# A tuned retention and SwiGLU kernel on one core: the last part of each h block moves from GpSimd to VectorE, the decays of k to ScalarE, and one silu into a PSUM bank

## The chip, the cores and the metric

The kernel runs on one core of a Trainium2 chip. The metric is the device time of one execution in microseconds (us). The kernel before was timed three times: 715.64, 715.67 and 717.3 us, median 715.67 us. One more execution was recorded by the hardware profiler; its span is 716.6 us, and all positions below ("at 374.96 us") count from the start of that span.

The engines are named as in the profile: PE is TensorE (its matmuls; PEld its weight loads), DVE is VectorE, ACT is ScalarE, POOL is GpSimd, SP issues most of the DMAs. Each engine works through its own instructions in order; semaphores tie the engines together.

## The reference

Two blocks, one behind the other, all in fp32.

```
B, H, S, D = 4, 8, 768, 64
gamma = 1 - 2 ** (-5 - h)                       # one decay per head
state = gamma * state + outer(k[t], v[t])       # per batch and head, D x D
y[t]  = (1 / sqrt(D)) * q[t] @ state            # over t = 0 .. S-1
x     = y as (B*S, H*D) = (3072, 512)
out   = (silu(x @ w_gate) * (x @ w_val)) @ w_out    # d_ff = 1536
```

## The kernel before

**Attention in chunks.** A sequence of 768 steps is cut into six chunks of 128. Inside a chunk the recurrence is a masked product of q and k, weighted by powers of gamma; between chunks a state of 64 x 64 per head is carried. For the state, k of the chunk is multiplied row by row by a decay that depends on the row and the head (`scale_k2`, the table `kdec`: 128 rows x 8 heads, each value good for 64 columns). For the part that reads the old state, q is multiplied by another table (`scale_q2`: one of the two chunks of a pair on VectorE, the other on GpSimd).

**Segments and stages.** The tokens are worked in four segments; a segment holds three chunks of each of two sequences, 768 tokens. A segment has an *up* stage (x times gate and value weights, silu, product: the hidden activations, kept transposed in `hT` as 12 blocks f of 128 rows x 2 x 384 tokens) and a *down* stage (the 12 blocks times w_out, summed up over f in six PSUM banks, one for each 128 tokens). Beside the matmuls of a down stage runs the attention of the next segment: three pairs of chunks p = 0, 1, 2, each with the parts s (scores, twice), m (mix with the own chunk), o (mix with the other half, then y is copied out of PSUM) and t (new state). The last down stage has no next segment.

**Parts of fp32.** Matmuls after the first up stage run on numbers rounded to a shorter mantissa. To keep fp32 accuracy each operand is split in three parts, and three passes are summed. A *near* split has three steps on three engines: `near_a` on ScalarE makes the rounded part, `near_b` on VectorE subtracts it from the operand, `near_c` on GpSimd adds the two parts into the third. It serves the weights of the up stages (`weights`) and the blocks of `hT` in the down stages (`h_split`). A *far* split (`far_a` to `far_d`) serves x and w_out; w_out is split once, in the first down stage (`w_load`, with `far_b` on GpSimd), and read back ready afterwards. The up product uses seven products instead of eight (a Strassen scheme over the two sequences, the two halves of d_model, and gate and value), which is why copies and sums of PSUM banks stand between the products.

**Order.** Nothing is scheduled by a machine at run time. Each step is entered with a due time, `at(t, fn, ...)`; `run` sorts all steps by due time and emits them in that order, so each engine's queue is the order of the due times. `down_stage` sets the due times of a down stage, `up3` those of an up stage from the second segment on. In `h_split` a block that TensorE needs at t has its three steps due at t - 7.5, t - 6.3 and t - 5.2.

**Lines that the change touches.** L538 is the POOL product of `scale_k2`. L663 is the POOL add of `near_c` (for weights and for h). L80 is the helper `both`, a VectorE instruction with two inputs; many steps are recorded there, the product `hT <- hT, tmp` of `up3` among them. `c11` in `up3` lies in `tmp` in SBUF; banks 0, 1, 6 and 7 are the PSUM banks that an up stage uses, banks 0 to 5 are those that a down stage sums in, 6 and 7 serve the attention.

Of the kernel before, what the change touches and what calls it, by code (L numbers as in the profile page):

```python
# [14 lines left out]
AF = mybir.ActivationFunctionType  # L15
ALU = mybir.AluOpType

P = 128
B, H, S, D = 4, 8, 768, 64
# [7 lines left out]
TH = L * P  # L27
# [18 lines left out]
ONE = 4095.0  # L46
# [3 lines left out]
def tile_retnet_swiglu(  # L50
# [22 lines left out]
    add, mul, sub = ALU.add, ALU.mult, ALU.subtract  # L73
    tt, stt, pool = (nc.vector.tensor_tensor, nc.vector.scalar_tensor_tensor,
                     nc.gpsimd.tensor_tensor)
    act, copy = nc.scalar.activation, nc.scalar.copy
# [8 lines left out]
    def f32(t):  # L85
        return t.bitcast(F32)
# [3 lines left out]
    hT = consts.tile([P, NF, 2, TH], F32, name="hT")  # L90
# [25 lines left out]
    banks = [psum.tile([P, 512], F32, name=f"bank{i}") for i in range(8)]  # L116
# [4 lines left out]
    def at(t, fn, *args, **kw):  # L121
        events.append((t, len(events), lambda: fn(*args, **kw)))  # L122
# [213 lines left out]
    kdec = tab[:, KDEC0:GDEC0]  # L336
# [90 lines left out]
    kdec_b = tab[:, ds(2 * TA, H)]  # L427
# [106 lines left out]

    def scale_k2(p, i):
        kd = given[p][3][i].rearrange("p (h d) -> p h d", h=H)
        dec = (kdec_b if i else kdec)[:, :, None].to_broadcast([P, H, D])
        pool(kd, kd, dec, op=mul)  # L538

    def new_states(s, p):  # L540
        ci = seg_chunks(s)[2 * p] % NCK
# [106 lines left out]
    def item(kind, n):  # L648
        k = turns[kind]
        turns[kind] += 1  # L650
        slots = {"g": 4, "o": 3}[kind]
        t = place(f"{kind}item{k}", {"g": 3 * 2 * TH, "o": 3 * DM}[kind], R12,
                  tag=f"{kind}{k % slots}")
        return t[:, : 3 * n].rearrange("p (a b) -> p a b", a=3)

    def near_a(o, x):
        act(o[0], x, AF.Copy, scale=CUT / FAR)  # L657

    def near_b(o, x):
        stt(o[1], f32(o[0]), -FAR, x, op0=mul, op1=add)  # L660

    def near_c(o):
        pool(o[2], f32(o[0]), f32(o[1]), op=add)  # L663

    def far_a(o, x):
        act(o[0], x, AF.Copy, scale=CUT)
# [10 lines left out]
    def near(t, o, x, n_a, n_b, n_c):  # L677
        o = o()
        at(t + n_a, lambda: near_a(o, x))
        at(t + n_b, lambda: near_b(o, x))  # L680
        at(t + n_c, lambda: near_c(o))
# [63 lines left out]
    def weights(t, f, g):  # L745
        it = {}
        if f == 0:
            t -= 1.8

        def begin():  # L750
            it["o"] = group(f, g)
            near_a(*it["o"])

        at(t - 7.2, begin)
        at(t - 5.6, lambda: near_b(*it["o"]))
        at(t - 4.4, lambda: near_c(it["o"][0]))
# [11 lines left out]
    def up3(s, f, t):  # L768
        x, z, wb = (banks[i][:, :TH] for i in (6 + f % 2, 0, 1))
        p1, u2, p5 = (tmp[:, ts(i, TH)] for i in range(3))  # L770
        c11 = tmp[:, ts(3 + f % 2, TH)]
        for g, first in enumerate((0, 3, 6)):
            weights(t + first * PROD, f, g)
        for n, p in enumerate(ORDER):
            o = {1: x, 6: x, 7: x, 4: x, 2: z, 5: wb, 3: wb}[p]
            at(t + n * PROD, product, s, f, p, o, p in (1, 2, 5))
        e = lambda n: t + (n + 1) * PROD + 0.1
        at(e(0), copy, p1, x)
        at(e(1), tt, c11, z, p1, op=add)
        at(e(1) + 0.7, act, c11, c11, AF.Silu, scale=ONE)  # L780
        at(e(2), copy, u2, x)
        at(e(3), copy, p5, wb)
        at(e(4), tt, hT[:, f, 1], x, p5, op=add)
        at(e(5), tt, hT[:, f, 0], wb, u2, op=add)
        at(e(5) + 0.7, both, hT[:, f, 0], hT[:, f, 0], c11, mul)
        at(e(6), act, x, x, AF.Silu, scale=ONE)
        at(e(6) + 0.7, tt, hT[:, f, 1], hT[:, f, 1], x, op=mul)

# [4 lines left out]
    def h_split(t, f):  # L793
        it = {}

        def begin():
            hs[f] = item("g", 2 * TH)
            it["o"] = [hs[f][:, i] for i in range(3)]
            near_a(it["o"], hT[:, f].rearrange("p i t -> p (i t)"))

        at(t - 7.5, begin)
        at(t - 6.3, lambda: near_b(it["o"], hT[:, f].rearrange("p i t -> p (i t)")))
        at(t - 5.2, lambda: near_c(it["o"]))

    def w_load(t, s, f):
        raw_w = chunk_x[:, ds(NC * 2 * P + f % 2 * DM, DM)]
# [50 lines left out]
    def down_stage(s, t, first_order=range(6), between=None):  # L857
        nxt = s + 1 if s + 1 < NSEG else None
        slot_at, steps = [], []
        for n in range(6 * NF):  # L860
# [4 lines left out]
            if nxt and n in PARTS:  # L865
# [3 lines left out]
                if what == "s":  # L869
                    at(t, scores_of, p, g)  # L870
                    for i in range(2):
                        at(d, decayed, p, g, i)
                    if g and ci:
                        for i in range(2):
                            at(d, scale_q2, p, i)
                elif what == "m":
                    at(t, mix_own, nxt, p)
                    at(d, fence)
                    if ci < NCK - 1:
                        for i in range(2):  # L880
                            at(d, scale_k2, p, i)
                elif what == "o":
                    at(t, mix_other, nxt, p)
                    if p == 0:
                        at(t, begin_x, nxt)
                    for c in range(2):
                        for i in range(2):
                            for hh in range(2):
                                at(d, bring_y, hh, i, c)
                    if ci < NCK - 1:  # L890
                        at(d + 2.4, decay2, nxt, p)
                    make_x(d + 2.6, nxt, p)
                elif ci < NCK - 1:
                    at(t, state2, nxt, p)
                    at(d, keep_state, nxt, p)
# [9 lines left out]
        for f in range(NF):  # L905
            h_split(steps[f], f)
            w_load(steps[f], s, f)
# [65 lines left out]
    t = down_stage(0, end, (0, 4, 3, 2, 5, 1), last_gates)  # L973
    for s in range(1, NSEG):
        for f in range(NF):
            up3(s, f, t + UPT * f)
            if f > 2:
                at(t + UPT * (f - 1) - 2.5, load_unit, f)
        t += NF * UPT
        if s + 1 < NSEG:  # L980
            for n in range(5):
                at(t - (18, 13, 12, 5, 4)[n], load_pair, s + 1, n)
        t = down_stage(s, t)
# [52 lines left out]
```

## Time and profile before

| what | before |
|---|---|
| time, median of 3 | 715.67 us |
| span of the profiled execution | 716.6 us |
| PE busy | 673.5 us (94%) |
| DVE busy | 496.8 us (69%) |
| ACT busy | 364.0 us (51%) |
| POOL busy | 355.9 us (50%) |
| mean granted TensorE clock | 0.982 of full speed |

How to read the profile's lines. A line of the table of stages gives a stretch in us, its length, the busy time and number of instructions of each engine in it, the granted TensorE clock, and the DMA. A line of the timeline gives start, duration, engine, line of the kernel, operation, output and inputs with their shapes, and in brackets how long the engine had been idle before it and who ended that. A line of the groups gives line, engine, operation, names, shapes, count, then busy time and mean duration in ns, then the idle time ahead of it. The first 143 us hold the attention of the first segment and its up stage, which the change does not touch; the four down stages begin near 143, 326, 493 and 663 us, the three later up stages near 240, 403 and 572 us.

### The profile page before, as it was taken

To read this page: it belongs to the slowest core of one execution; us is meant where nothing else is said; L and a number is where in the kernel's file an instruction comes from. 1 tells how busy PE (TensorE), PEld (TensorE's weight loads), DVE (VectorE), ACT (ScalarE), POOL (GpSimd) and SP (SyncE) were. 2 spreads that over 40 slices of the span, in tenths; PEclk is the share of its full clock that TensorE was granted. 3 is DMA by queue.
4 is the path that set the end of the run, shared out by engine and by line. 5 is a ranking of instruction groups with operands and counts; after the bars stand their busy time and mean duration, and the time that the engine had idled before them with its cause. 6 is when DMAs were issued, how large, how long until landed. Compare 5 with 4: busy or idle time off the path is not lost.

```text
span 716.6 us, 12389 instructions
## 1 busy us (share of the span) xinstructions
PE 673.5 (94%) x4724; PEld 553.9 (77%) x4724; DVE 496.8 (69%) x730; ACT 364.0 (51%) x693; POOL 355.9 (50%) x226
## 2 busy tenths in 40 slices
PE   7998999997878999999989899999998899999997
PEld 6754555566666899997667799998776699999886
DVE  3888998777788676774765767766566766777421
ACT  2668787525646555551545554553442655554211
POOL 0434444565745555664345555554453455665540
PEclk9999999999989999999999999999999999999999
DMA  9796898966565533265765443254755544232564
GB/s 313 255 371 223 239 394 346 291 241 206 189 228 207 192 114 144 87 217 162 248 206 206 157 148 110 102 184 151 235 183 191 192 160 141 103 103 88 178 202 150
DMA packets 51739, 140.80 MB, mean 196 GB/s; under 512 B 6368, under 2 KB 19168, under 8 KB 51680
## 3 DMA queue, kind: packets, MB, share of 16 engines
q1 hardware_dynamic: 48224, 133.72, 54.5%
q10 hardware_dynamic: 3456, 6.29, 2.5%
q8 instruction: 37, 0.61, 0.4%
q14 instruction: 22, 0.18, 0.1%
HBM read 110.11 MB, written 29.88 MB: 195 GB/s over the span
## 4 chain that ended last, share of the span: by engine, by line
PE 68%; DVE 13%; ACT 6%; issue 4%; POOL 3%; DMA 1%; ACTq 0%; SPq 0%; DVEq 0%; POOLq 0%
PE bank L764 36%; PE bank L830 15%; PE bank L600 12%; PE bank L458 5%; ACT chunk_x L695 3%; DVE x L80 3%; DVE gitem L660 2%; DVE tmp L80 2%; DVE x L672 1%; ACT gitem L657 1%; POOL gitem L663 1%; POOL first L252 1%; DVE chunk_x L841 1%; DMA loads<-in_k_n_dram 1%; DVE tmp L477 1%
## 5 line engine op out<-in xcount | busy, mean ns | idle before, releaser
L663 POOL TENSOR_TENSOR gitem<-gitem 128x768 fp32r<-128x768 f32 x120 | 228.1, 1901 | 183.7 <-DVE gitem L660 170.7
L764 PE MATMUL bank<-x,gitem 128*128 128x384 f32 x1296 | 239.8, 342 | 6.7 <-ACT tmp L122 6.2
L764 PEld LDWEIGHTS bank<-x,gitem 128*128 128x128 f32 x1296 | 226.0, 190 | 15.3 <-ACT tmp L122 7.9
L830 PE MATMUL bank<-oitem,gitem 128*128 128x512 f32 x864 | 216.4, 405 | 3.8 <-ACT oitem L675 3.2
L830 PEld LDWEIGHTS bank<-oitem,gitem 128*128 128x128 f32 x864 | 162.9, 193 | 43.2 <-issue 6.5
L660 DVE SCALAR_TENSOR_TENSOR gitem<-gitem,loads 128x768 fp32r<-128x768 f32 x72 | 81.2, 1127 | 60.9 <-ACT gitem L657 60.9
L600 PE MATMUL bank<-first 128*128 128x384 f32 x336 | 111.2, 489 | 2.6 <-DVE hT L635 1.6
L600 PEld LDWEIGHTS bank<-first 128*128 128x128 f32 x336 | 62.8, 190 | 49.0 <-DVE hT L635 2.2
L660 DVE SCALAR_TENSOR_TENSOR gitem<-gitem,hT 128x768 fp32r<-128x768 f32 x48 | 55.8, 1164 | 46.4 <-ACT gitem L657 46.2
L252 POOL TENSOR_TENSOR first<-first,rawp 128x1024 int32<-128x1024 int32 (+1 forms) x21 | 40.0, 1919 | 58.5 <-DVE first L242 31.5
L657 ACT ACTIVATE gitem<-loads 128x768 fp32r<-128x768 f32 x72 | 60.7, 843 | 2.9 <-DVE oitem L660 2.9
L122 ACT ACTIVATE bank<-bank 128x384 f32<-128x384 f32 x36 | 17.1, 475 | 73.8 <-PE bank L764 73.8
L695 ACT COPY chunk_x<-bank 64x256 f32<-64x256 f32 x72 | 26.4, 367 | 54.3 <-PE bank L458 53.4
L122 ACT COPY tmp<-bank 128x384 f32<-128x384 f32 x108 | 50.6, 469 | 3.7 <-PE bank L764 3.6
L657 ACT ACTIVATE gitem<-hT 128x768 fp32r<-128x768 f32 x48 | 39.5, 836 | 25.0 <-PE bank L830 24.9
L122 DVE TENSOR_TENSOR hT<-bank,tmp 128x384 f32<-128x384 f32 x72 | 39.8, 554 | 17.3 <-PE bank L764 17.3
L764 PE MATMUL bank<-x,oitem 128*128 128x384 f32 x216 | 44.8, 342 | 0.4 <-DVE hT L122 0.4
L458 PEld LDWEIGHTS bank<-loads 64*64 64x64 f32 (+1 forms) x800 | 23.9, 141 | 26.1 <-DVE tmp L477 12.4
L122 ACT ACTIVATE tmp<-tmp 128x384 f32<-128x384 f32 x36 | 18.9, 526 | 48.7 <-DVE tmp L122 48.7
L458 PE MATMUL bank<-loads 64*64 64x64 f32 (+2 forms) x800 | 29.0, 253 | 15.0 <-DVE tmp L477 8.6
L663 POOL TENSOR_TENSOR oitem<-oitem 128x256 fp32r<-128x256 f32 x36 | 26.6, 739 | 30.5 <-DVE oitem L660 30.5
L764 PEld LDWEIGHTS bank<-x,oitem 128*128 128x128 f32 x216 | 36.3, 188 | 3.3 <-DVE hT L122 0.7
(97 smaller groups left out, 699.6 us busy)
## 6 DMA issues: line engine op xcount, KB each, us to landing
loads<-wup SPq DMA_DIRECT2D x36, 896.0 KB, 4.7
oitem<-wdnt SPq DMA_DIRECT2D x36, 768.0 KB, 4.4
wup<-first SPq DMA_DIRECT2D x12, 896.0 KB, 8.8
wdnt<-oitem SPq DMA_DIRECT2D x12, 768.0 KB, 4.5
rawp<-in_w_val_dram SPq DMA_DIRECT2D x24, 256.0 KB, 5.8
rawp<-in_w_gate_dram SPq DMA_DIRECT2D x12, 512.0 KB, 6.5
out_dram<-chunk_x ACTq DMA_DIRECT2D x24, 256.0 KB, 2.1
loads<-in_k_t_dram SPq DMA_DIRECT2D x18, 256.0 KB, 3.7
```

The lines of the kernel that those rows point to most:

```text
L80: stt(o, x, 1.0, y, op0=mul, op1=op)
L122: events.append((t, len(events), lambda: fn(*args, **kw)))
L252: pool(d[:, ts(i, n)].bitcast(I32), d[:, ts(i, n)].bitcast(I32), lo[:, ts(i, n)].bitcast(I32), op=add)
L458: nc.tensor.matmul(o, a, b, start=start, stop=True, skip_group_check=True)
L477: tt(att[p, g, i], banks[R0 + i][:, :TA], side[g][:, i], op=mul)
L600: nc.tensor.matmul(o, w[:, slot, k], a[:, k], start=(start and k == 0), stop=(stop and k == KH - 1), skip_group_check=True)
L657: act(o[0], x, AF.Copy, scale=CUT / FAR)
L660: stt(o[1], f32(o[0]), -FAR, x, op0=mul, op1=add)
L663: pool(o[2], f32(o[0]), f32(o[1]), op=add)
L695: copy(cx[half[i], ds(2 * h, 2), c], y_both(h, i, c))
L764: nc.tensor.matmul(o, w[:, a, k], xs_of[s][:, a, OP[p], k], start=start and a == k == 0, stop=a == 2 and k == KH - 1, skip_group_check=True)
L830: nc.tensor.matmul(banks[tok], hs[f][:, a, ds(i * TH + u * P, P)], wo[f][:, a], start=f == a == 0, stop=f == NF - 1 and a == 2, skip_group ...
```

## The change

It makes three edits.

1. The third step of each split of an h block (`near_c` in `h_split`) runs on VectorE instead of GpSimd, and is due 0.1 us earlier. There are 12 blocks in each of four down stages, 48 in all. For the weights it stays on GpSimd.
2. The decays of k (`scale_k2`) become eight ScalarE copies with a per-row scale, one for each head, instead of one GpSimd product; 14 products become 112 copies.
3. In the later up stages silu of `c11` writes into a PSUM bank that the stage does not use (banks 2 and 3, in turn for even and odd f), and the product that follows reads it from there. Before, silu was written over `c11` in SBUF, and the product had both inputs in SBUF.

The purpose is to take work off GpSimd, and to have fewer VectorE instructions that read two operands from SBUF.

```diff
     def scale_k2(p, i):
         kd = given[p][3][i].rearrange("p (h d) -> p h d", h=H)
-        dec = (kdec_b if i else kdec)[:, :, None].to_broadcast([P, H, D])
-        pool(kd, kd, dec, op=mul)
+        dec = kdec_b if i else kdec
+        for h in range(H):
+            act(kd[:, h], kd[:, h], AF.Copy, scale=dec[:, ds(h, 1)])
...
-    def near_c(o):
-        pool(o[2], f32(o[0]), f32(o[1]), op=add)
+    def near_c(o, op=pool):
+        op(o[2], f32(o[0]), f32(o[1]), op=add)
...
         c11 = tmp[:, ts(3 + f % 2, TH)]
+        gate = banks[2 + f % 2][:, :TH]
...
-        at(e(1) + 0.7, act, c11, c11, AF.Silu, scale=ONE)
+        at(e(1) + 0.7, act, gate, c11, AF.Silu, scale=ONE)
...
-        at(e(5) + 0.7, both, hT[:, f, 0], hT[:, f, 0], c11, mul)
+        at(e(5) + 0.7, tt, hT[:, f, 0], hT[:, f, 0], gate, op=mul)
...
-        at(t - 5.2, lambda: near_c(it["o"]))
+        at(t - 5.3, lambda: near_c(it["o"], both))
```

## The prediction

> **What bounds the kernel now.** I read the busy times first, then a table by stage, then the PE timeline of the down stages for its idle time, and last the DVE and POOL timelines at those moments. Busy time on the page:
>
> ```profile
> PE 673.5 (94%) x4724; PEld 553.9 (77%) x4724; DVE 496.8 (69%) x730; ACT 364.0 (51%) x693; POOL 355.9 (50%) x226
> ```
>
> TensorE leaves 43 us, of which 5 are start-up (25.80 busy of the first 31 us). The table by stage says where the rest is:
>
> ```profile
> 143.00:240.00 97.00, 82.21 (x797) 63.42 (x796) 75.29 (x91) 49.75 (x95) 56.60 (x35) 0.93 0.62 217
> 240.00:326.00 86.00, 85.63 (x481) 81.92 (x480) 62.11 (x93) 44.58 (x92) 49.34 (x34) 1.00 0.42 143
> 326.00:403.00 77.00, 71.30 (x772) 55.28 (x770) 50.43 (x69) 34.97 (x68) 37.00 (x22) 1.00 0.59 197
> 493.00:572.00 79.00, 72.86 (x772) 56.39 (x770) 53.24 (x70) 33.95 (x66) 35.45 (x20) 0.98 0.55 188
> ```
>
> The up stages (second row) are full: PE 85.63 of 86, nothing to win there. The first three down stages, D0, D1 and D2, have 14.8, 5.7 and 6.1 us of idle PE. That is the most an edit of the other engines can give, apart from a slower clock behind long stalls. In D1 the PE timeline shows each stall with who ended it:
>
> ```profile
> 328.19 0.99 PE L458 MATMUL bank<-loads 64*64 64x128 f32 x30 [0.60 <-DVE hT L122]
> 352.26 1.35 PE L458 MATMUL bank<-loads 64*64 64x128 f32 x32 [0.94 <-DVE tmp L477]
> 358.12 0.55 PE L458 MATMUL bank<-loads,states 64*64 64x128 f32 x11 [0.52 <-POOL loads L531]
> 374.96 1.35 PE L458 MATMUL bank<-loads 64*64 64x128 f32 x32 [1.89 <-DVE tmp L477]
> ```
>
> These are attention parts that wait for DVE to empty a bank (L477), or for the scaled q (L531). DVE does it late because it is held in the instruction before. Ahead of the 374.96 stall:
>
> ```profile
> 371.58 2.86 DVE L80 SCALAR_TENSOR_TENSOR x<-x,tmp 128x1024 fp32r<-128x1024 f32 x1
> 374.36 1.01 DVE L477 TENSOR_TENSOR tmp<-bank,tab 128x384 f32<-128x384 f32 x2
> 371.47 1.89 POOL L663 TENSOR_TENSOR gitem<-gitem 128x768 fp32r<-128x768 f32 x1 [6.15 <-DVE gitem L660]
> ```
>
> The same L80 form has a median of 1.22 us; here it takes 2.86, as it began 0.11 us after a POOL add and ran on its own pace once that ended at 373.36. So a POOL instruction costs DVE up to its whole duration. A stall of 1.9 to 3.8 us is also followed by a slow clock; for the one at 543.52 us in D2:
>
> ```profile
> 540.00:545.00 5.00, 3.07 (x40) 2.11 (x38) 5.00 (x5) 0.42 (x1) 1.88 (x1) 0.95 0.71 231
> 545.00:551.00 6.00, 6.00 (x54) 4.73 (x55) 2.79 (x5) 2.52 (x3) 3.14 (x2) 0.76 0.46 151
> ```
>
> At 0.76 for 6 us some 1.4 us of matmul work are lost on top of the 1.90 us stall.
>
> **What the Trainium skill says.** "SBUF — State Buffer", section "Who interferes with whom": "A DVE instruction with two SBUF inputs contends with a GpSimd instruction that reads SBUF", and the second to issue is fully blocked. The trace agrees: the product hT <- hT,tmp (L80, both inputs in SBUF) takes 557 ns at its least and 1031 in the mean, while the same 384 columns with one input in PSUM (L122) take 542, and 555 at most. "ScalarE: Activation LUTs", section "What ACT_TABLE_LOAD costs", prices an ACTIVATE at 186 ns + 0.833 per column, + 93 for a per-row operand, with 93 ns of overlap back to back: for 64 columns 332 and a pitch of 239. The trace has this form at L380, 334 ns; its pitch is seen at L549 (128 columns, 389 ns, four in 1.28 us: 297), which less 64 x 0.833 gives 244. "TensorE: Matmul & The Clock Gate", part 1, puts the clock at half after an idle window of about 3.4 us; the trace has dips already behind 1.90 us, so I take its own.
>
> **The change, part by part.**
>
> *near_c of h on DVE.* It removes 48 POOL adds of 1.84 us (12 a stage) and adds 48 DVE instructions of 768 columns with two SBUF inputs; the equal form is near_b (L660), 0.95 us, 0.88 as pitch since neighbours overlap. So DVE gets 12 x 0.88 = 10.5 us more in a stage. What it gets back is the blocking by those adds: in D1 the excess over the least duration of each form is 1.5 (345.86), 0.5 (355.52), 1.1 (356.86), 0.6 (360.04), 1.6 (371.58), 0.3 (381.81), 1.1 (390.61), together 6.7 us. DVE busy in D1 rises from 50.4 to about 54 of 77 us: not a bound. What matters is where the instructions stand ahead of a stall. From the instruction order of the changed kernel, stall by stage:
> D1: at 328.19 two near_c stand shortly ahead of the last product of the up stage, one of them directly, against a product at 325.76 that took 1.91 and will take 0.55 (edit 3): -0.5. At 352.26 the burst loses 1.54 and gets one near_c of 0.88: -0.7. At 358.12 the scaled q waited behind a POOL near_c of 2.71, gone: -0.5. At 374.96 the L80 loses 1.64, and the near_c of that block is queued behind L477, not ahead: -1.6. Sum -3.3.
> D2 has the same four (0.62; 1.30 behind the new state; 0.51; 1.90): -0.5, -0.7, -0.5, -1.65, and without the last stall the clock dip of 1.4 should go: -4.7.
> D0 keeps 12 POOL adds for w_out (L669), which go on blocking. Stalls 3.55, 1.59, 1.13, 3.83 and 3.23 us: the first is neutral (1.5 of blocking less at 169.37, 0.88 of near_c and up to 0.8 of ScalarE delay more), then -0.7, -0.8, -1.6 (L80 at 200.56 took 2.82, with near_c again behind L477), -0.7. The dip behind the fourth, 0.62 over 9 us or 3.4 us of work, may shrink: I take -1.2. At the start of D0 near_c of block 0 now stands in DVE's queue ahead of L635 and L638, for which a product waits: +0.7. Sum -4.3.
> D3 has no attention and a full PE: 0.
> The wait that each near_c adds is for near_b just ahead on the same engine; behind it are the sums of x, then L477 and the new state, for which PE waits; counted above.
>
> *Decays on ScalarE.* 7 pairs of chunks x 16 copies x 0.244 = 3.9 us of ScalarE each, 27 us in all (between 239 and 334 ns a copy: 27 and 37). POOL loses 14 x 1.365 = 19 us. They stand behind a near_a, ahead of the y copies (L695). Before those ScalarE idles 12.8, 5.9 and 5.8 us in D1, 13.6 and 5.9 in D2, and 4.0 us before the far_d at 188.29 in D0: there they are hidden at no cost. Two tight places: D0, first pair, y copies 0.8 us later (counted), and D1, third pair, where k is issued at 376.4 to 377.9 and lands (median 4.0 us) near 381.5, with copies to about 384.3 and a near_a behind, against 384.86: 0 to 1 us, I take 0.
>
> *silu into PSUM.* Silu costs 482 instead of 526 ns (the first up stage has the form bank<-tmp, L612); the product 0.55 instead of 1.03, 36 times, 17 us of DVE in full up stages: nothing on the path but the 0.5 counted. Banks 2 and 3 are free there: the last product is read before the down stage reaches its fourth token block (329 us against 326.3).
>
> The sum is -12.3, 703.4 us. Removed stalls rarely come in full, as PE arriving earlier meets the next wait (transfers, y copies), and the two down-to-up turns (2.41 and 2.96 us of stall) hang on a DVE burst whose length stays (-1.07 +0.88). I take three quarters: -9.2, **706.5 us**.
>
> **Rivals.**
> *A, full gain or more* (chance 0.22): all dips but those at the turns go, D0's fourth stall with them: 715.7 - 12.3 - 3 = 700.4 us. For it: the dips follow stalls that lose most of their length. Against: D0's keep 2 us and more.
> *B, little moves* (0.16): the stalls are ended by something else right behind, y copies or far_d: the two L477 stalls of D1 and D2 alone give -3.5: 712 us. For it: ACT's waits in D0 (28.2 us for DVE at L675) remain. Against: at 374.96 nothing but DVE's queue holds PE.
> *C, slower* (0.07): near_c is on the path in each of the nine attention pairs, 9 x 0.88 = 8 us, of which relief pays 4, and the ScalarE copies delay y by 1 us in two: 715.7 + 8 - 4 + 2 = 722 us. For it: DVE is already busy 6 of 7 us around the stalls. Against: four of the stalls have it behind L477.
> *The forecast* has 0.55.
>
> **How the numbers follow.** Faster by over 0.3% means under 713.5: the forecast, A, and most of B, 0.55 + 0.22 + 0.10 = 0.87; same 0.06 from the rest of B; slower 0.07 from C. The range leaves out the far half of A and all of C: 700.5 to 714 us.
>
> **What would show it.** POOL busy down by about 48 x 1.9 + 19 = 110 us to 246; DVE about 48 x 0.95 - 17 - 20 (three stages like D1's 6.7) = 9 up, near 505; ACT 35 up. L80 hT gone as a group, its successor at 0.55 us. L80 x<-x,tmp at 1.22 in D1 and D2. PE idle under 3 us in D1 before the turn; no dip in D2 before 560 us. It is wrong if L477 or the new state still holds PE for over 1 us in D1 and D2 (rival C, or B if near_c is not what stands before it), or if L695 starts over 1 us after its part o.

## The result, and the profile after

| | before | after |
|---|---|---|
| median of 4 runs, same chip | 716.48 us (715.64 to 717.88) | 704.96 us (704.16 to 707.31) |
| ratio, 95% interval | | 0.9843 [0.9812, 0.9873] |
| span of the profiled execution | 716.6 us | 702.4 us |

The changed kernel is 1.6% faster. The two profiled executions lie further apart (14.2 us) than the medians (11.5 us): by the timer, the profiled execution of the kernel before took 718.37 us, above its median, and that of the changed kernel 704.16, its shortest. Their mean granted clocks, 0.982 and 0.989, lie further apart than those of the timed runs too (median 0.986 over 19 further runs of the kernel before, 0.985 to 0.989 in the four of the changed one). Shares of stages below are read from the profiles, gains of versions from the timed runs.

Busy times, from the page of the changed kernel:

```profile
PE 664.6 (95%) x4724; PEld 552.3 (79%) x4724; DVE 496.8 (71%) x778; ACT 391.4 (56%) x805; POOL 247.9 (35%) x164
```

GpSimd loses 108 us. VectorE has 48 instructions more and is busy for exactly as long as before. TensorE has the same 4,724 matmuls, and is "busy" 8.9 us less.

The table by stage of the changed kernel (stretch, length, then PE, PEld, DVE, ACT, POOL, granted clock, DMA), D0, D1, D2:

```profile
143.00:236.00 93.00, 80.11 (x794) 60.78 (x793) 77.10 (x103) 57.05 (x127) 28.64 (x19) 0.96 0.65 225
322.00:396.00 74.00, 70.33 (x769) 54.62 (x767) 52.93 (x80) 46.52 (x116) 9.46 (x5) 1.00 0.61 207
486.00:560.00 74.00, 69.42 (x767) 54.32 (x766) 53.09 (x80) 40.81 (x97) 10.73 (x6) 1.00 0.60 203
```

In D1 and D2 GpSimd has 5 and 6 instructions left, of 22 and 20. Idle PE in D1 is 3.7 us where it was 5.7, and half of that is the turn into the next up stage. The stalls of D1, from the PE timeline:

```profile
346.54 1.35 PE L458 MATMUL bank<-loads 64*64 64x128 f32 x32 [0.28 <-DVE tmp L477]
352.62 0.67 PE L458 MATMUL bank<-loads,states 64*64 64x128 f32 x16 [1.10 <-DVE loads L80]
367.81 1.35 PE L458 MATMUL bank<-loads 64*64 64x128 f32 x32 [0.25 <-DVE tmp L477]
```

They answer one by one to the lines of before: 0.60 gone, 0.94 now 0.28, 0.52 now 1.10 and ended by VectorE instead of GpSimd, 1.89 now 0.25. The groups of the changed kernel that the edits touch:

```profile
L80 DVE SCALAR_TENSOR_TENSOR gitem<-gitem 128x768 fp32r<-128x768 f32 x48 | 51.4, 1072 | 1.0
L539 ACT ACTIVATE loads<-loads,tab 128x64 f32<-128x64 f32 x112 | 27.5, 334 | 0.9 <-DMA loads<-in_k_n_dram 0.9
L80 DVE SCALAR_TENSOR_TENSOR x<-x,tmp 128x1024 fp32r<-128x1024 f32 x9 | 11.0, 1218 | 0.0
```

The last row is the held instruction of the prediction. The same row in the kernel before:

```profile
L80 DVE SCALAR_TENSOR_TENSOR x<-x,tmp 128x1024 fp32r<-128x1024 f32 x9 | 15.8, 1761 | 0.0
```

Its mean fell from 1761 ns to the undisturbed 1218. The 72 adds that GpSimd keeps are those of the weights.

The length of each stage, taken from the starts of its first matmul and of the next stage's first, says where the 14.2 us are:

| us | D0 | U1 | D1 | U2 | D2 | U3 | one block in the middle of U | last block of U |
|---|---|---|---|---|---|---|---|---|
| before | 89.28 | 91.32 | 73.36 | 93.75 | 75.07 | 95.14 | 7.50 | 7.4 to 7.5 |
| after | 85.46 | 90.37 | 70.79 | 92.66 | 70.93 | 93.43 | 7.29 to 7.31 | 8.0 to 8.1 |

Down stages: 10.5 us. Up stages: 3.75 us, where none had been expected. The first 145 us and the last down stage differ by 0.1 us together.

Part of the 10.5 us is TensorE's clock. Multiplied by the length of its stretch, what the granted clock lacks to 1.00 in the tables by stage is 6.8 us in D0 and 1.6 in D2 before, and 3.7 and 0 after. So up to 4.7 us of these two gains (an estimate from the tables) come from fewer spells of slow clock. D1 has none in either kernel; its 2.6 us are shorter waits alone.

### The profile page after: what moved, and what is told of

Same layout as the page of the kernel before. It is cut to its first block, busy times and chain, and to the rows that moved or that the text cites. A ratio compares the mean times of both kernels' runs of the same rounds, so it can differ in the third digit from the quotient of the medians.

```text
span 702.4 us, 12451 instructions
## 1 busy us (share of the span) xinstructions
PE 664.6 (95%) x4724; PEld 552.3 (79%) x4724; DVE 496.8 (71%) x778; ACT 391.4 (56%) x805; POOL 247.9 (35%) x164
## 4 chain that ended last, share of the span: by engine, by line
PE 63%; DVE 16%; ACT 8%; DMA 6%; issue 4%; SPq 1%; POOL 0%; ACTq 0%; DVEq 0%; POOLq 0%
PE bank L765 35%; PE bank L832 15%; PE bank L601 9%; PE bank L458 4%; DVE gitem L661 3%; ACT chunk_x L696 3%; DVE x L673 2%; DVE x L80 2%; ACT gitem L658 2%; DVE gitem L80 1%; DVE tmp L80 1%; DMA loads<-in_v_n_dram 1%; DVE tmp L477 1%; DVE first L80 1%; DMA rawp<-in_q_t_dram 1%
## 5 line engine op out<-in xcount | busy, mean ns | idle before, releaser
L765 PE MATMUL bank<-x,gitem 128*128 128x384 f32 x1296 | 235.4, 338 | 7.5 <-ACT tmp L122 7.5
L832 PE MATMUL bank<-oitem,gitem 128*128 128x512 f32 x864 | 213.7, 401 | 4.2 <-ACT oitem L676 2.9
L832 PEld LDWEIGHTS bank<-oitem,gitem 128*128 128x128 f32 x864 | 160.7, 190 | 43.2 <-issue 4.5
L664 POOL TENSOR_TENSOR gitem<-gitem 128x768 fp32r<-128x768 f32 x72 | 135.6, 1883 | 128.0 <-DVE gitem L661 128.0
L661 DVE SCALAR_TENSOR_TENSOR gitem<-gitem,loads 128x768 fp32r<-128x768 f32 x72 | 74.0, 1027 | 68.2 <-ACT gitem L658 68.2
L661 DVE SCALAR_TENSOR_TENSOR gitem<-gitem,hT 128x768 fp32r<-128x768 f32 x48 | 47.9, 997 | 48.0 <-ACT gitem L658 48.0
L531 POOL TENSOR_TENSOR loads<-loads,tab 128x512 f32<-128x512 f32 x8 | 13.8, 1729 | 110.9 <-PE bank L458 110.9
L80 DVE SCALAR_TENSOR_TENSOR gitem<-gitem 128x768 fp32r<-128x768 f32 x48 | 51.4, 1072 | 1.0
L122 DVE TENSOR_TENSOR hT<-hT,bank 128x384 f32<-128x384 f32 x72 | 39.8, 553 | 5.1 <-ACT bank L122 1.5
L122 ACT ACTIVATE bank<-tmp 128x384 f32<-128x384 f32 x36 | 17.9, 496 | 43.8 <-DVE tmp L122 43.8
```

Source lines behind the costliest of these rows:

```text
L80: stt(o, x, 1.0, y, op0=mul, op1=op)
L664: op(o[2], f32(o[0]), f32(o[1]), op=add)
L765: nc.tensor.matmul(o, w[:, a, k], xs_of[s][:, a, OP[p], k], start=start and a == k == 0, stop=a == 2 and k == KH - 1, skip_group_check=True)
L832: nc.tensor.matmul(banks[tok], hs[f][:, a, ds(i * TH + u * P, P)], wo[f][:, a], start=f == a == 0, stop=f == NF - 1 and a == 2, skip_group ...
```

## The experiments

The first four kernels start from the kernel before and hold a part of the change each; the other four start from the changed kernel. Ratios are to the kernel before, on the same chip (medians 717.64 us of 19 runs for the first four, 717.73 of 17 for the others).

**The h blocks alone (edit 1).**

```diff
-    def near_c(o):
-        pool(o[2], f32(o[0]), f32(o[1]), op=add)
+    def near_c(o, op=pool):
+        op(o[2], f32(o[0]), f32(o[1]), op=add)
...
-        at(t - 5.2, lambda: near_c(it["o"]))
+        at(t - 5.3, lambda: near_c(it["o"], both))
```

> Only near_c of h on VectorE; decays of k and silu as before. Theory 1 (VectorE was held by the reads of GpSimd's near_c): the three attention down stages lose most of what they lost in the changed kernel, about 8 of 10.4 us, the up stages lose nothing and pay some 0.5 us each at their end: ratio 0.988 to 0.992, about 708 us against 716.5. Theory 2 (the decays of k on GpSimd, two in a row of 2.8 us, are what held it): under 2 us of gain, ratio over 0.997.

Measured: 711.06 us, 0.9907 [0.9890, 0.9925]. D1 by the PE timeline of this kernel, with the end of U1 ahead of it:

```profile
319.90 2.35 PE L764 MATMUL bank<-x,gitem 128*128 128x384 f32 x12 [1.54 <-ACT tmp L122]
...
348.63 1.35 PE L458 MATMUL bank<-loads 64*64 64x128 f32 x32 [0.28 <-DVE tmp L477]
354.71 0.67 PE L458 MATMUL bank<-loads,states 64*64 64x128 f32 x16 [1.08 <-DVE loads L80]
369.91 1.36 PE L458 MATMUL bank<-loads 64*64 64x128 f32 x32 [0.24 <-DVE tmp L477]
```

The down stages are those of the whole change: D0, D1, D2 are 85.66, 70.83 and 70.94 us. So this edit alone makes nearly all of the 10.5 us there (10.3), and also the new 1.1 us stall. The up stages grow by 1.9 us in sum: the last block takes 8.4 to 9.1 us (the longest has the first line's stall of 1.54 us in it), while the blocks in the middle stay at 7.50. By the timed runs the edit is worth 6.6 us.

**The silu alone (edit 3).**

```diff
+        gate = banks[2 + f % 2][:, :TH]
...
-        at(e(1) + 0.7, act, c11, c11, AF.Silu, scale=ONE)
+        at(e(1) + 0.7, act, gate, c11, AF.Silu, scale=ONE)
...
-        at(e(5) + 0.7, both, hT[:, f, 0], hT[:, f, 0], c11, mul)
+        at(e(5) + 0.7, tt, hT[:, f, 0], hT[:, f, 0], gate, op=mul)
```

> Only silu of c11 into a PSUM bank and the product that reads it from there. Theory 1 (the small waits of 0.02 to 0.1 us inside the blocks of the up stages, at products 5, 6 and 7, come from VectorE being held in this product): each block of 42 matmuls goes from 7.50 to about 7.31 us, 36 blocks, 5 to 7 us in all, ratio 0.990 to 0.993. Theory 2, the step of the prediction (up stages are full, only the last product of a stage counts): 1 us, ratio 0.998 to 1.000, blocks stay at 7.5 us.

Measured: 710.07 us, 0.9897 [0.9872, 0.9921], 7.4 us, about as much as the other edit. The up stages lose 6.5 us in the profile (89.58, 90.98, 93.17): 5.5 in the blocks behind the first of each stage, and 0.9 in the first block of U2, where this profile has no spell of slow clock. A block of this kernel's U2, from the PE timeline, begins with each of the lines of 36 matmuls (the second is cut by the end of the window), so it runs from the first start to the last:

```profile
429.77 6.41 PE L764 MATMUL bank<-x,gitem 128*128 128x384 f32 x36
...
437.05 4.15 PE L764 MATMUL bank<-x,gitem 128*128 128x384 f32 x23
```

That is 7.28 us. The same in the kernel before, with VectorE and ScalarE beside it:

```profile
432.58 1.02 DVE L80 SCALAR_TENSOR_TENSOR hT<-hT,tmp 128x384 f32<-128x384 f32 x1
432.87 6.60 PE L764 MATMUL bank<-x,gitem 128*128 128x384 f32 x36
...
435.50 0.54 DVE L122 TENSOR_TENSOR tmp<-bank,tmp 128x384 f32<-128x384 f32 x1
436.51 0.46 ACT L122 COPY tmp<-bank 128x384 f32<-128x384 f32 x1
```

and in the changed kernel:

```profile
424.91 0.56 DVE L122 TENSOR_TENSOR hT<-hT,bank 128x384 f32<-128x384 f32 x1
425.16 6.41 PE L765 MATMUL bank<-x,gitem 128*128 128x384 f32 x36
...
427.50 0.56 DVE L122 TENSOR_TENSOR tmp<-bank,tmp 128x384 f32<-128x384 f32 x1
428.53 0.48 ACT L122 COPY tmp<-bank 128x384 f32<-128x384 f32 x1
```

Count from the start of each 36. The held product (1.02 against 0.56, first line) pushes what follows on VectorE, where a `near_b` is then held in its turn (1.24 for 0.96 us, from 434.33): the sum that makes `c11` ends at 3.17 us instead of 2.90, ScalarE's silu of it and the copy of a bank behind that end at 4.10 instead of 3.85. TensorE needs that bank for the fifth product, and waits for about 0.1 us. The starts of single matmuls in the trace show longer gaps behind matmuls 25, 31 and 37 of the 42 of a block: all that exceeds the median gap of 173 to 174 ns adds up to 1.5 to 1.6 us in eight blocks before, 0.2 to 0.5 after. The timeline joins them into one line of 36 and the table counts them as busy, because the ends of matmuls are modelled. A window of the kernel before:

```profile
280.00:300.00 20.00, 20.00 (x114) 19.10 (x113) 14.69 (x22) 10.56 (x22) 12.05 (x9) 1.00 0.28 93
```

PE 20.00 of 20, and yet the stage was not full. The weight loads say it: 19.10 us here, 19.66 in the same window with this edit. Only the distance of the blocks shows the size.

The edit changes two things at once, the product and silu's destination, and the kernel before can tell them apart. The second block of U2, from its timeline:

```profile
410.37 0.56 DVE L80 SCALAR_TENSOR_TENSOR hT<-hT,tmp 128x384 f32<-128x384 f32 x1
410.63 6.40 PE L764 MATMUL bank<-x,gitem 128*128 128x384 f32 x36
413.56 0.53 ACT L122 ACTIVATE tmp<-tmp 128x384 f32<-128x384 f32 x1 [1.15 <-DVE tmp L122]
417.94 2.24 PE L764 MATMUL bank<-x,gitem 128*128 128x384 f32 x12
```

Here the product happened not to be held (0.56), silu wrote to SBUF as ever, and the block took 7.31 us. The second blocks of U1 and U3 took 7.30 and 7.29. So it is the late end of the held product that costs, not silu, which the new destination shortens by only 0.03 us (526 to 496 ns in the mean).

**Both, with the decays left on GpSimd (edits 1 and 3).**

```diff
-        dec = kdec_b if i else kdec
-        for h in range(H):
-            act(kd[:, h], kd[:, h], AF.Copy, scale=dec[:, ds(h, 1)])
+        dec = (kdec_b if i else kdec)[:, :, None].to_broadcast([P, H, D])
+        pool(kd, kd, dec, op=mul)
```

(shown against the changed kernel)

> Changed kernel with the decays of k back on GpSimd. Theory 1 (decays are nearly free on either engine): within 2 us of the changed kernel, ratio 0.982 to 0.987. Theory 2 (the GpSimd decays hold VectorE in front of a wait of TensorE): ratio 0.989 or more, with PE stalls over 1 us behind DVE in D1 or D2 where POOL runs the decays.

Measured: 704.75 us, 0.9820 [0.9803, 0.9838]. The interval overlaps that of the whole change. The two edits together give a little less than their sum (0.93% and 1.03%, together 1.80%), and they account for the whole change.

**The decays alone (edit 2)**, the diff above the other way round, in the kernel before.

> Only the decays of k as ScalarE copies. Theory 1: nothing measurable, ratio 0.997 to 1.001, since near_c still holds VectorE at the same places. Theory 2 (the ScalarE copies delay the copies of y): ratio 1.002 to 1.008, with L695's successor starting over 1 us after its part o.

Measured: 718.92 us, 1.0014 [1.0001, 1.0028], between the ranges of the two theories: a loss of about 1 us, at the edge of what these runs can tell. One new stall is in its D0, where `scale_k2` stands ahead of the y copies of the first pair:

```profile
165.34 1.15 PE L458 MATMUL bank<-loads 128*64 128x64 f32 x32 [0.80 <-ACT chunk_x L696]
```

It is the 0.8 us that had been counted; the rest of the 27 us of ScalarE work is hidden. With edits 1 and 3 or without them, this edit gains nothing that these runs can tell.

**The adds back on GpSimd, for nobody.** In D1 and D2 GpSimd makes the old add for blocks 0 to 9 besides, into a part of `chunk_x` that nothing reads.

```diff
+        if s in (1, 2) and f < 10:
+            at(t - 5.2, lambda: pool(chunk_x[:, ds(1024, 768)], f32(it["o"][0]),
+                                     f32(it["o"][1]), op=add))
```

> Changed kernel, and in down stages D1 and D2 a GpSimd add of the old form and size beside ten of the twelve h blocks; it reads the same two parts and writes to an unused part of chunk_x, so that nobody needs its result. Theory 1 (VectorE is held by what GpSimd reads): D1 and D2 get 2.5 to 5 us longer each (70.8 and 70.9 us before), forms of L80 and L673 over twice their least duration again, 710 to 714 us, ratio 0.991 to 0.997. Theory 2 (the gain came from parts of h being ready sooner and GpSimd's queue being short for the scaled q): under 1.5 us in all, ratio under 0.987.

Measured: 716.19 us, 0.9986 [0.9969, 1.0002]; all that the change had brought is gone, which is beyond the ranges of both theories. D1 and D2 take 77.13 and 77.08 us, 6.3 and 6.2 more than in the changed kernel. Each holds two spells of slow clock in this profile, the slowest of the twelve runs, and up to 3.4 us of it are that; what is left fits the 2.5 to 5 us expected. Nor is it a plain return to the kernel before: VectorE still makes every `near_c` itself, and is held besides (busy for 509.7 us, where both other kernels have 496.8). The stall of before is back; from the timeline of this kernel:

```profile
372.30 1.88 POOL L807 TENSOR_TENSOR chunk_x<-gitem 128x768 f32<-128x768 f32 x1 [5.04 <-DVE gitem L661]
372.41 2.86 DVE L80 SCALAR_TENSOR_TENSOR x<-x,tmp 128x1024 fp32r<-128x1024 f32 x1
...
375.79 1.81 PE L458 MATMUL bank<-loads 64*64 64x128 f32 x32 [1.89 <-DVE tmp L477]
```

Again 0.11 us between the start of the add and that of the L80, again 2.86 us for 1.22, again 1.89 us of PE. Nobody waits for the add's result; it costs by running beside VectorE. That it is the reads, the next kernel shows.

**The same place, with GpSimd only writing.** The add is cut to one column (it keeps the wait for `near_b`) and a fill of the other 1,023 columns follows.

```diff
+            at(t - 5.2, lambda: pool(chunk_x[:, ds(1024, 1)], f32(it["o"][0])[:, :1],
+                                     f32(it["o"][1])[:, :1], op=add))
+            at(t - 5.2, lambda: nc.gpsimd.memset(chunk_x[:, ds(1025, 1023)], 0.0))
```

> The same, with a GpSimd fill of 1023 columns in place of the add: it writes SBUF and reads only one column ahead of it. Theory 1 in its narrow form (only reads hold VectorE): D1 and D2 within 1 us of the changed kernel, ratio 0.981 to 0.986. Rival (any use of the shared SBUF ports by GpSimd holds VectorE): D1 and D2 1 to 4 us longer, as for the add, scaled by the duration of the fill.

Measured: 702.98 us, 0.9799 [0.9774, 0.9824], just below the range of the narrow theory. GpSimd is busy 28 us more than in the changed kernel, and D1 and D2 are 0.9 us shorter, not longer. The same VectorE instruction of D1, two inputs in SBUF and 256 columns, begins in both kernels while GpSimd is at work. Beside the add, in the kernel above:

```profile
344.68 1.89 POOL L807 TENSOR_TENSOR chunk_x<-gitem 128x768 f32<-128x768 f32 x1 [7.90 <-DVE gitem L661]
344.90 1.95 DVE L80 SCALAR_TENSOR_TENSOR tmp<-tmp,chunk_x 128x256 f32<-128x256 f32 x1
```

and beside the fill, in this one:

```profile
339.84 0.95 POOL L809 MEMSET chunk_x<- 128x1023 f32 x1
339.89 0.43 DVE L80 SCALAR_TENSOR_TENSOR tmp<-tmp,chunk_x 128x256 f32<-128x256 f32 x1
```

It takes 1.95 us in the one and 0.43 in the other. The Trainium skill, "SBUF — State Buffer", section "Who interferes with whom", says that a VectorE instruction with two inputs in SBUF contends with a GpSimd instruction that reads SBUF, "not with one that only writes it"; these two runs agree.

Why the stages got shorter is seen at the scaled q. First the wait in the changed kernel, from its timeline:

```profile
347.97 1.99 POOL L531 TENSOR_TENSOR loads<-loads,tab 128x512 f32<-128x512 f32 x1 [33.42 <-PE bank L458]
348.73 2.31 DVE L673 SCALAR_TENSOR_TENSOR x<-x 128x1024 fp32r<-128x1024 f32 x1
...
351.89 0.68 DVE L80 SCALAR_TENSOR_TENSOR loads<-loads,tab 128x512 f32<-128x512 f32 x1
```

GpSimd has idled for 33 us and so takes up its half of the scaled q (L531) as soon as the scores release it. That holds VectorE's L673 for 2.31 us instead of 1.22, and VectorE's own half of the scaled q (351.89) comes 1.1 us late to TensorE. In the kernel with the fills:

```profile
347.82 1.22 DVE L673 SCALAR_TENSOR_TENSOR x<-x 128x1024 fp32r<-128x1024 f32 x1
347.88 0.95 POOL L809 MEMSET chunk_x<- 128x1023 f32 x1
348.80 1.40 POOL L531 TENSOR_TENSOR loads<-loads,tab 128x512 f32<-128x512 f32 x1
350.81 0.67 PE L458 MATMUL bank<-loads,states 64*64 64x128 f32 x16 [0.18 <-DVE loads L80]
```

The whole fill lies within L673 and does not hold it. It only keeps L531 back until L673 is nearly done, and the stall of 1.10 is 0.18.

**The first two h blocks back on GpSimd.** In the changed kernel, at the end of U1, from its timeline:

```profile
313.09 4.33 PE L765 MATMUL bank<-x,gitem 128*128 128x384 f32 x24
315.39 0.96 DVE L80 SCALAR_TENSOR_TENSOR gitem<-gitem 128x768 fp32r<-128x768 f32 x1
316.27 0.55 DVE L122 TENSOR_TENSOR tmp<-bank,tmp 128x384 f32<-128x384 f32 x1
...
317.81 2.37 PE L765 MATMUL bank<-x,gitem 128*128 128x384 f32 x12 [0.40 <-ACT tmp L122]
321.09 1.55 PE L832 MATMUL bank<-oitem,gitem 128*128 128x512 f32 x6
```

The last up block (313.09 to 321.09) takes 8.00 us, 0.55 more than before the change: the `near_c` of the first h block stands ahead of the `c11` sum on VectorE, silu and the copies on ScalarE follow late, and TensorE waits for a copy. There is no attention at that place for the edit to relieve.

```diff
-        at(t - 5.3, lambda: near_c(it["o"], both))
+        at(t - 5.3, lambda: near_c(it["o"], both if f > 1 else pool))
```

> Changed kernel with near_c of the first two h blocks of each down stage back on GpSimd. Theory (the wait of about 0.4 us in the last block of an up stage and the one of 1.0 us at the start of D0 come from these two near_c in VectorE's queue): last blocks go from 8.0 to 7.3 us, the start of D0 loses 0.8 us, together 2 to 3 us, ratio 0.977 to 0.982. Rival: the two additions on GpSimd hold VectorE at the first L477 of the stage and take it back: no gain, 0.982 to 0.986.

Measured: 698.61 us, 0.9740 [0.9719, 0.9761], more than was expected. The end of U1 in this kernel:

```profile
311.47 6.40 PE L765 MATMUL bank<-x,gitem 128*128 128x384 f32 x36
...
318.76 1.55 PE L832 MATMUL bank<-oitem,gitem 128*128 128x512 f32 x6
...
393.36 4.45 PE L765 MATMUL bank<-x,gitem 128*128 128x384 f32 x24 [2.20 <-ACT tmp L122]
```

The block takes 7.29 us, and the stall is gone; so is the 1.02 us that TensorE waited at the start of D0 of the changed kernel for the same reason (0.23 here). The last line belongs to the next paragraph. Summed over stages, this profile has 3.5 us less in the up stages than the changed kernel and 2.3 us less in the down stages. Of the up part 2.1 us are the last blocks (three of 8.0 against 7.3); the other 1.4 are about what the clock differs in U2, below. Of the down part 0.8 are the start of D0; the rest was not traced further.

**Three further moves of due times** on top of that one: the two late steps of a large x split 2.4 us later for the first two pairs, and the weights of the first two up blocks nearer to their use or on VectorE, aimed at the scaled q and at the turns from down to up.

```diff
-            (0.2, 2.0, 2.6, 3.4), (0.9, 3.2, 3.6, 4.2), (1.6, 3.9, 6.6, 8.0)]
+            (0.2, 2.0, 2.6, 3.4), (0.9, 3.2, 3.6, 4.2), (1.6, 3.9, 9.0, 10.4)]
...
-        at(t - 7.2, begin)
-        at(t - 5.6, lambda: near_b(*it["o"]))
-        at(t - 4.4, lambda: near_c(it["o"][0]))
+        at(t - (5.9 if f == 1 and g == 0 else 7.2), begin)
+        at(t - (5.0 if f == 1 and g == 0 else 5.6), lambda: near_b(*it["o"]))
+        at(t - (5.5 if f == g == 0 else 4.4), lambda: near_c(it["o"][0], both if f == g == 0 else pool))
```

> As p_4, and three more moves in the order: the last big step of the x split (L673, 1024 columns) behind the second L477 pair in the first two parts; near_a of the first group of block 1 behind the first copy of an up stage; near_c of the first weight group of an up stage on VectorE. Theory: the wait for the scaled q in D1 and D2 (1.1 us each) and D0 shrinks, the stall at the turns from down to up goes from 2.2 and 3.3 us to under 1.9, and with it the slow clock behind it: 6 to 9 us less than the changed kernel, ratio 0.970 to 0.976. Rival: ScalarE's output transfers ahead of the first copy still wait for VectorE, turns keep 2 us: 2 to 4 us, 0.977 to 0.981.

Measured: 697.52 us, 0.9723 [0.9702, 0.9744], within the range of the theory, but it can't be told from the version before it. From the PE timeline at the end of its D1:

```profile
367.03 1.35 PE L458 MATMUL bank<-loads 64*64 64x128 f32 x32 [1.00 <-DVE tmp L477]
...
395.06 4.43 PE L765 MATMUL bank<-x,gitem 128*128 128x384 f32 x24 [1.57 <-ACT tmp L122]
```

The 1.10 at the scaled q is gone and the turn's stall fell from 2.20 to 1.57, but 0.75 us came back at the L477 wait and a new wait of 1.18 stands behind the turn (at 400.67). In the main, waits were moved, not removed. The two last kernels are the best of this study; both beat the change as it was made.

## Why the prediction was right, and where it was not

The time, 704.96 us, lies 1.5 us under the forecast of 706.5 and inside the range, and its main mechanism stood. The terms were not all right, and the total fits so well in part by luck. By the timed runs edit 1 is worth 6.6 us and edit 3 7.4; the sum had given edit 3 at most 1.0 (twice the 0.5) and edit 1 the other 11.3, 8.5 after the discount. Too much on the one and far too little on the other cancelled.

| step | predicted, us | by the two profiles |
|---|---|---|
| D0 | -4.3 | -3.8 |
| D1 | -3.3 | -2.6 |
| D2 | -4.7 | -4.1 |
| up stages | 0 | -3.75 |
| sum | -12.3 | -14.3 (medians of the timed runs: -11.5) |
| taken | three quarters, -9.2 | |

The right column holds what the clock happened to do in the two profiles, in D0 and D2 above all. Only D1 compares waits alone: 2.6 us where 3.3 had been worked out.

*VectorE held by GpSimd's adds*: right, and shown, not only argued. Taking the adds away brings L80 from 1761 to 1218 ns in the mean and D1's two L477 stalls from 0.94 and 1.89 to 0.28 and 0.25; putting them back for nobody brings stalls (1.81 and 1.89) and the time back; a fill in their place does not. The signs named in advance came out as well: GpSimd 247.9 us (246), 1.8 us of idle PE in D1 before the turn (under 3), no wait of over 0.64 us for L477 or the new state in D1 and D2, no slow clock in D2, and the y copies of D1 at most 0.6 us behind their part o.

*The stalls of D1 one by one*: three of four as worked out. "At 358.12 the scaled q waited behind a POOL near_c of 2.71, gone: -0.5" failed. That add is gone, but the engine it had kept busy now begins its next instruction early and holds VectorE with it: 1.10 us instead of 0.52, in D1 and D2 alike. The step looked at who would stop waiting and not at whom the freed engine would meet.

*D0*: the first stall, taken as neutral, went from 3.55 to 2.80; the fourth from 3.83 to 1.56, and its slow clock went with it, though a spell of 3.4 us came behind the second (1.50, at 184.03); the start of D0 lost 0.8 (a wait of 1.02 us for 0.24), where 0.7 had been counted. Two new waits of 0.82 and 0.70 took a part back.

*The turns* keep their stalls, as was said: 2.41 and 2.96 became 2.20 and 3.26.

*The step that failed: "The up stages (second row) are full: PE 85.63 of 86, nothing to win there", and from it "nothing on the path but the 0.5 counted" for the silu.* Edit 3 alone is worth 1.03%, half of everything, and most of it in the blocks of the up stages: 0.2 us in each block of 7.5. A busy share of PE near 100% does not tell a full engine from one that waits for less than 0.1 us at a time. Had the blocks' distance been read (7.50 us for 42 matmuls, 178.6 ns each, where the second block of each stage already took 7.30 us, or 173.8 ns), the room would have been seen.

*The near_c of blocks 0 and 1* were counted at the start of D0, and at 328.19 set against the shorter product. They also stand ahead of the `c11` sum in the last block of every up stage, and cost about 0.55 us in each there.

*The decays*: rightly costed at nothing. ACT rose by 27.4 us. The working had said 27 (37 without overlap of neighbouring copies), and the 35 among the signs did not follow from it.

*VectorE's busy time* was forecast to rise by 9 us and did not rise. Edit 1 gave +22.2 (25.6 worked out), edit 3 gave -20.1 (17 worked out); taking the decays off GpSimd gave VectorE 6.4 us back (503.2 with edits 1 and 3, 496.8 with all), which had not been counted.

*The discount of a quarter* was argued from stalls that give way to the next wait. That happened (1.10, 0.82, 0.70, the last up blocks), and it was too small for edit 1 alone: 6.6 of 11.3. Rivals B and C are refuted by the stage lengths: D1 and D2 did not end on other waits, and the nine attention pairs did not lose time. Rival A fails too: D0 keeps a spell of slow clock away from the turn, and the time is 4.6 us above its 700.4.

*The slow clock*: "a stall of 1.9 to 3.8 us is also followed by a slow clock" was read too simply. The prediction's own table has a clock of 1.00 for D1, with a stall of 1.89 us in it. Whether a dip comes is worked out in the last section; that the one in D2 went, as counted, fits it, since no wait that long is left there.

## What to carry to other kernels

When a transfer of work takes an engine's load away, look up its next instruction and ask whom it will now meet, as well as who stops waiting for it. A stage whose PE is busy 99% of the time is not proved full: compare the distance of its repeated blocks with the number of matmuls in them times the shortest pitch in the trace. And where an edit is made in a loop, test its first and last rounds apart: the same move that paid in ten of the twelve h blocks cost time in the first two.

## What the hardware showed that was not expected

**The slow clock goes by windows of 3.41 us that the kernel does not set.** The same stall of 2.20 us at the turn from D1 to U2 was followed by slow clock in the changed kernel:

```profile
396.35 6.01 PE L765 MATMUL bank<-x,gitem 128*128 128x384 f32 x24 [2.20 <-ACT tmp L122]
...
393.32:396.73 3.41, 1.21 (x7) 0.89 (x6) 2.23 (x3) 1.81 (x3) 1.90 (x2) 1.00 0.72 228
396.73:400.14 3.41, 3.41 (x13) 3.41 (x12) 1.17 (x3) 1.72 (x3) 1.82 (x1) 0.50 0.71 273
```

and by none in the version with two blocks on GpSimd, where the same 24 matmuls took 4.45 us (their line, at 393.36, stands above):

```profile
388.80:392.21 3.41, 2.36 (x14) 2.00 (x12) 2.99 (x4) 1.13 (x3) 2.18 (x2) 1.00 0.47 175
392.21:395.62 3.41, 2.26 (x13) 2.26 (x14) 1.43 (x2) 2.29 (x5) 1.93 (x2) 1.00 1.01 336
```

In the records of all ten profiles the granted clock is full or half, nothing between. A slow spell lasts 3.41 us or twice that (a spell at the very end of the kernel apart), and within one profile the spells begin whole multiples of 3.41 us apart. So I cut each profile into windows of that length, in step with its slow spells. In the changed kernel the whole stall lies in one window, PE is busy for 1.21 of 3.41 us (35%), and the next window runs at half clock. In the other kernel an edge of the windows divides the stall, PE is busy for 69% and 66% of the two, and the clock stays full.

The count over the ten profiles has 1,989 windows at full clock. In 47 of them PE was busy for 44% or less, and each was followed by a slow one; in 1,930 it was busy for 54% or more, and none was. The 12 between went either way (5 slow). PE's busy time is modelled, so these shares are rough. This fits what else was seen: the stall of 1.89 us in D1 was followed by full clock in the kernel before and by slow clock in the kernel with edit 3 alone, in D2 it was the other way round (1.90 with a dip, 1.87 without), and in D0 of the changed kernel even 2.80 us, most of it in a window 47% busy, were followed by full clock.

The Trainium skill, "TensorE: Matmul & The Clock Gate", part 1, ties the drop to an idle window of about 3.4 us and calls that window free-running. The traces agree with the length and with the free running, but a window need not be idle: 44% of work in it was not enough to keep the clock.

What is chance is where the windows fall on a stall. A spell costs up to 1.7 us (half of 3.41), so a single profile of such a kernel can be off by several of these, and only the timed runs say what a version is worth.

**A fill by GpSimd was free to VectorE**, whichever began first: 0.95 us for 1,023 columns, beside two-input VectorE instructions that took their undisturbed 0.43 us (fill first) and 1.22 us (L673 first). An add by GpSimd holds VectorE, and is held by it: where such an add began 0.11 us behind a `near_c` of VectorE, it took 2.5 us in place of 1.84.
